# GpSimd's sums of the attention's P in instructions of 224 columns in place of 448

## The chip, the cores and the metric

The kernel runs on one core of a Trainium2 chip. The metric is the device time of one execution in microseconds; several executions are timed and their median is given. One execution was profiled, and the views below come from that one.

## What is computed

Three layers follow one another: attention with capped scores, a soft mixture of experts, and a two-layer MLP. The change lies in the attention.

```python
# q, k, v: (4, 12, 448, 64)   batch, heads, sequence, head size
scores = scale * np.matmul(q, k.transpose(0, 1, 3, 2))
scores = cap * np.tanh(scores / cap)
scores = scores - np.max(scores, axis=-1, keepdims=True)
attn = np.exp(scores)
attn = attn / (np.sum(attn, axis=-1, keepdims=True) + 1e-09)
attn_out = np.matmul(attn, v)
...
x = attn_out.transpose(0, 2, 1, 3).reshape(1792, 768)
x = soft_moe(x, phi, w1, w2)       # 8 experts of 4 slots, 768 -> 1024 -> 768
out = mlp(x, w_in, w_out, alpha)   # 768 -> 2048 -> 768, leaky rectifier
```

## The kernel before

**Attention.** The 48 heads are worked off as 24 pairs (`NPAIR`), i = 0 to 23. P is kept transposed, keys on the partitions and the 448 queries along the columns. The 448 keys are cut into three chunks of 128 (c = 0, 1, 2) and a tail of 64 (c = 3), whose two heads share one tile of 128 partitions. The order of the chunks is `CHUNKS = (0, 3, 1, 2)`.

The loop runs over steps g, four to a pair. In step g `qk` makes the scores of one chunk on TensorE (tile `s`, three products of a high and a low part) and ScalarE turns them into P: tanh (L408) and exp (L409), for both heads at once, 896 columns. Two steps later (`LAG = 2`) `pv` multiplies that P with V (tile `o`). Between them the background work of the step is issued (`run_bg`): row sums, normalisation, logits of the mixture, and so on.

**The sums of P.** The softmax needs the sum of P over all keys. GpSimd adds the chunks into a tile `acc` of 128 partitions, two heads `u` and 448 columns (`S`); `acc` has one buffer for even and one for odd pairs. In `pv` with c = 1 it adds chunks 0 and 1 (L425) and then the tail (L428, 64 partitions); with c = 2 it adds chunk 2 (L432). That is six instructions of 448 columns for a pair, and two for the last pair, whose other parts TensorE adds. `row_sums` (L440 on) then sums `acc` over the partitions with matmuls against `hot`, four calls of 224 columns (`HS`), two heads times two halves, into a tile `rs`; they are issued two steps after `pv` with c = 2. VectorE adds `rs` into `sums` (L459, L463), and after three pairs takes the reciprocal and splits it (L487 to L489), from which TensorE spreads `rb` and VectorE makes the normalised output `xn` out of `xu` (L513).

**What else VectorE does there.** For every pair it makes the parts of Q and K: `qh` (L387), `kl` (L374), `ql` (L388). For the MLP's weights `w_in`, which come as 64-bit numbers, it does a conversion in `to_f32` once in about four steps: ScalarE begins it (L203) and VectorE does four steps in place on 512 columns of `cvbuf`, L204, L208, L211 and L214; where they fall is set by a table of steps:

```python
cv_steps = [2, 5] + list(range(9, 58, J)) + [59] + list(range(61, 90, J))   # J = 4
```

For each batch (six pairs) it makes the softmax over slots, with a subtraction and a product in `c_all` (L694, L699) around an exp on ScalarE (L695).

**What sets the order.** TensorE's matmuls are chained in the order of the program text. The other engines' instructions are placed by the framework's scheduler out of the same text; each engine works its own list in order, and semaphores join them. GpSimd has nothing else to do in the attention but the sums.

**After the attention** come the experts, whose weights arrive by DMA from about 235 us on, and from about 330 us the MLP on TensorE.

Of the kernel before, what the change touches and what calls it, by code (L numbers as in the profile page):

```python
# [25 lines left out]
def tile_attention_soft_moe_mlp(ctx, tc, q, k, v, cap, phi, w1, w2, w_in, w_out, alpha, out):  # L26
    nc = tc.nc
    B, H, S, D = q.shape
# [12 lines left out]
    HS = S // 2  # L41
# [4 lines left out]
    JK = 3  # L46
# [205 lines left out]
    def attention():  # L252
        with ExitStack() as pools:
# [43 lines left out]
            nat, stk, sc_t, pt, acc, ov, xu, xn = {}, {}, {}, {}, {}, {}, {}, {}  # L297
# [7 lines left out]
            def matmul(*a, **kw):  # L305
                ins = nc.tensor.matmul(*a, **kw)  # L306
                if order:
                    if order[0] is not None:
                        tc.add_manual_dep(ins.ins, order[0].ins.name, NOSYNC, reason="tilings together")
                    order[0] = ins  # L310
                return ins
# [5 lines left out]
            def later(d, fn, *a):  # L317
                bg.setdefault(now[0] + d, []).append((fn, a))
# [93 lines left out]
            def pv(i, c):  # L412
                if c == 0:
                    ov[i] = ps_o.tile([128, 512], F32, tag="o", name="o")
                    acc[i] = acc_p[i % 2].tile([128, 2, S], F32, tag="acc", name="acc")
                o, a, t, pe = ov[i], acc[i], nat["v", i], pt[i, c]
                if i == NPAIR - 1 and c == 2:
                    row_sums(i)
                for u in range(2):
                    r = slice(TAIL * u, TAIL * u + TAIL)  # L420
                    lhsT, rhs = (t[r, 2 * JK, :], pe[r, 0, :]) if c == JK else (t[:, JK * u + c, :], pe[:, u, :])
                    matmul(o[64 * u:64 * u + 64, :S], lhsT, rhs, start=(c == 0), stop=(c == 2))
                if c == 1:
                    for u in range(2):
                        nc.gpsimd.tensor_add(out=a[:, u, :], in0=pt[i, 0][:, u, :], in1=pe[:, u, :])  # L425
                        r = slice(TAIL * u, TAIL * u + TAIL)
                        if i < NPAIR - 1:
                            nc.gpsimd.tensor_add(out=a[r, u, :], in0=a[r, u, :], in1=pt[i, JK][r, 0, :])  # L428
                if c == 2:
                    if i < NPAIR - 1:  # L430
                        for u in range(2):
                            nc.gpsimd.tensor_add(out=a[:, u, :], in0=a[:, u, :], in1=pe[:, u, :])  # L432
                    xu[i] = xu_p.tile([128, J * 128], F32, tag="xu", name="xu")[:, :S]
                    nc.scalar.activation(out=xu[i], in_=o[:, :S], func=AF.Copy)  # L434
                    if i < NPAIR - 1:
                        later(2 if i < NPAIR - 2 else 1, row_sums, i)
# [321 lines left out]
            for g in range(NPAIR * J + LAG):  # L758
                now[0] = g
                i, c = divmod(g, J)  # L760
                if g == 14:
                    nc.sync.dma_start(out=alpha_sb, in_=alpha.rearrange("(k p) -> p k", p=128))
                if g == 17:
                    nc.vector.tensor_scalar(out=nalpha_sb, in0=alpha_sb, scalar1=-1.0, scalar2=None, op0=ALU.mult)
                if i < NPAIR:
                    qk(i, CHUNKS[c])
                    if c == 1 and i + 1 < NPAIR:
                        trans_k(i + 1)
                        trans_q(i + 1)
                run_bg()  # L770
                if i < NPAIR:
                    if c == 0:
                        last = load(i + 2, "kq") or last
                    for n in range(ncv):
                        if cv_at(n) == g - 2:
                            store_w_in(n)
                        if cv_at(n) == g:
                            conv_w_in(n)
                if g >= LAG:
                    n, e = divmod(g - LAG, J)  # L780
                    pv(n, CHUNKS[e])
                    if e == J - 1:
                        load(n + 2, "v")
                if i < NPAIR and c == 1 and i in LOADS and may_load() is not None:
                    load_next(last)
            while bg:
# [10 lines left out]
                out=diag, in0=stackI[:, 0:NSLOT], scalar1=z_run, scalar2=None, op0=ALU.mult  # L797
# [668 lines left out]
```

## Time and profile before

| | |
|---|---|
| median of 3 runs | 583.16 us (581.52 to 583.71) |
| the profiled execution | 583.41 us, its span 581.6 us |
| TensorE busy | 550.8 us, 95% of the span |
| VectorE busy | 425.9 us, 73% |
| ScalarE busy | 387.3 us, 67% |
| GpSimd busy | 173.4 us, 30% |
| chain of waits, largest shares | TensorE 71%, DMA 14%, ScalarE 7%, VectorE 5% |
| granted TensorE clock | full in all of 40 slices |

In the profile PE is TensorE, DVE is VectorE, ACT is ScalarE, POOL is GpSimd and SP is SyncE. A share of the whole span says little here, since the three layers have different limits: GpSimd's 30% lie almost all in the first 248 us. A row of the timeline may stand for several like instructions (x2); its time is then from the first one's start to the last one's end. In brackets stands the idle time of the engine ahead of it and what ended it.

### The profile page before, as it was taken

The numbers are of one execution on the slowest core, as the hardware profiler recorded it, in microseconds if no ns is written. First come the engines' busy times: TensorE is split into PE (matmuls) and PEld (weight loads), VectorE is DVE, ScalarE is ACT, GpSimd is POOL, SyncE is SP. The second block draws the span as 40 slices with busy tenths as digits, with TensorE's granted clock in tenths as the row PEclk, the third lists the DMA queues.
The fourth block names the chain that finished last, engine by engine and source line by source line (L and its number), as shares of the span: only waits on it lengthen the run. The fifth ranks groups of instructions, "written<-read, shape, count | busy, mean of one in ns | idle before, by whom it ended". The sixth has DMA issues, their size and how long they took to land.

```text
span 581.6 us, 11121 instructions
## 1 busy us (share of the span) xinstructions
PE 550.8 (95%) x4204; PEld 388.7 (67%) x4204; DVE 425.9 (73%) x782; ACT 387.3 (67%) x612; POOL 173.4 (30%) x158
## 2 busy tenths in 40 slices
PE   5999999999999999999997899999999999999996
PEld 4444444455444544466664567878888999999996
DVE  3778767796999768661023379998999979797974
ACT  3999989898988878721012368985777755555551
POOL 0798786767595755600000000000000000000000
PEclk9999999999999999999999999999999999999999
DMA  7668788887878992899999999300120101010101
GB/s 176 155 134 252 215 256 260 259 257 205 256 218 222 319 280 58 310 398 415 419 414 420 389 395 416 141 1 1 54 56 1 54 2 55 1 55 2 54 1 54
DMA packets 83604, 110.93 MB, mean 191 GB/s; under 512 B 55392, under 2 KB 63328, under 8 KB 82016
## 3 DMA queue, kind: packets, MB, share of 16 engines
q1 hardware_dynamic: 81312, 109.28, 56.2%
q10 hardware_dynamic: 2240, 0.95, 0.6%
q8 instruction: 33, 0.54, 0.4%
q14 instruction: 19, 0.16, 0.1%
HBM read 98.41 MB, written 11.80 MB: 190 GB/s over the span
## 4 chain that ended last, share of the span: by engine, by line
PE 71%; DMA 14%; ACT 7%; DVE 5%; issue 1%; SPq 1%; ACTq 0%; DVEq 0%
PE o L306 10%; DMA w<-in_moe_w_dram 9%; PE s L306 9%; PE P L1280 7%; PE P L1278 7%; PE P L1279 7%; PE oc L1052 6%; PE oc L1053 6%; PE oc L1046 6%; DMA v<-in_v_dram 3%; PE aps L974 2%; PE nx L306 2%; ACT p L408 2%; ACT p L409 2%; PE rs L306 2%; PE tr L306 1%
## 5 line engine op out<-in xcount | busy, mean ns | idle before, releaser
L306 PE MATMUL o<-p,v 128*64 128x448 f32 (+1 forms) x384 | 93.3, 564 | 6.7 <-ACT xu L434 4.0
L408 ACT ACTIVATE p<-s 128x896 f32<-128x896 f32 x96 | 78.8, 821 | 22.6 <-PE s L306 19.6
L409 ACT ACTIVATE p<-p,cap 128x896 f32<-128x896 f32 x96 | 90.9, 948 | 2.3
L425 POOL TENSOR_TENSOR acc<-p 128x448 f32<-128x448 f32 x48 | 61.6, 1304 | 57.5 <-ACT p L409 57.4
L1052 PE MATMUL oc<-wsp,gr 128*128 128x512 f32 (+1 forms) x192 | 65.0, 339 | 0.3 <-DVE wsp L866 0.3
L1053 PE MATMUL oc<-wsp,gr 128*128 128x512 f32 (+1 forms) x192 | 64.3, 338 | 0.0
L1046 PE MATMUL oc<-wsp,gr 128*128 128x512 f32 (+1 forms) x192 | 63.7, 340 | 0.0
L306 PEld LDWEIGHTS s<-qh,kh 64*128 64x128 f32 (+1 forms) x168 | 18.2, 186 | 66.6 <-issue 25.4
L1269 ACT ACTIVATE gr<-gs 128x384 fp32r<-128x384 f32 (+1 forms) x64 | 36.8, 577 | 33.8 <-DVE gs L1253 27.8
L428 POOL TENSOR_TENSOR acc<-acc,p 64x448 f32<-64x448 f32 x46 | 55.4, 1205 | 1.7
L432 POOL TENSOR_TENSOR acc<-acc,p 128x448 f32<-128x448 f32 x46 | 53.4, 1181 | 1.8
L1270 DVE TENSOR_TENSOR gr<-gs,gr 128x384 fp32r<-128x384 f32 x64 | 39.1, 619 | 18.1 <-ACT gr L1269 18.1
L306 PE MATMUL s<-qh,kh 64*128 64x448 f32 (+1 forms) x168 | 46.0, 476 | 0.0
L1278 PE MATMUL P<-wsp,gr 128*128 128x384 f32 x128 | 42.9, 335 | 0.0
L1279 PE MATMUL P<-wsp,gr 128*128 128x384 f32 x128 | 42.8, 334 | 0.0
L1280 PE MATMUL P<-wsp,gr 128*128 128x384 f32 x128 | 42.8, 334 | 0.0
L1046 PEld LDWEIGHTS oc<-wsp,gr 128*128 128x128 f32 x192 | 36.3, 190 | 5.5 <-issue 0.6
L1052 PEld LDWEIGHTS oc<-wsp,gr 128*128 128x128 f32 x192 | 36.4, 189 | 5.2 <-DVE wsp L866 0.8
L306 PEld LDWEIGHTS o<-p,v 128*64 128x64 f32 (+1 forms) x384 | 19.0, 134 | 31.2 <-ACT xu L434 11.2
L1053 PEld LDWEIGHTS oc<-wsp,gr 128*128 128x128 f32 x192 | 36.3, 189 | 5.1 <-issue 0.8
L306 PE MATMUL s<-ql,kh 64*128 64x448 f32 (+1 forms) x168 | 35.6, 368 | 1.1 <-DVE ql L388 1.1
L306 PE MATMUL s<-qh,kl 64*128 64x448 f32 (+1 forms) x168 | 35.6, 367 | 0.0
(230 smaller groups left out, 1226.0 us busy)
## 6 DMA issues: line engine op xcount, KB each, us to landing
w<-in_moe_w_dram SPq DMA_DIRECT2D x25, 768.0 KB, 10.4
w<-in_moe_w_dram SPq DMA_DIRECT2D x12, 1536.0 KB, 11.3
cvbuf<-in_moe_w_in_dram SPq DMA_DIRECT2D x24, 512.0 KB, 5.5
w<-in_moe_w_out_dram SPq DMA_DIRECT2D x16, 768.0 KB, 10.8
w_in<-cvbuf SPq DMA_DIRECT2D x24, 256.0 KB, 3.3
w<-in_moe_w_dram SPq DMA_DIRECT2D x12, 512.0 KB, 6.4
w<-in_moe_w_dram SPq DMA_DIRECT2D x14, 384.0 KB, 4.9
q<-in_q_dram SPq DMA_DIRECT2D x44, 112.0 KB, 3.6
```

The costliest lines, as they stand in the source:

```text
L306: ins = nc.tensor.matmul(*a, **kw)
L408: nc.scalar.activation(out=pe, in_=ps[:, :n, :S], func=AF.Tanh)
L409: nc.scalar.activation(out=pe, in_=pe, func=AF.Exp, scale=cap_sb)
L425: nc.gpsimd.tensor_add(out=a[:, u, :], in0=pt[i, 0][:, u, :], in1=pe[:, u, :])
L428: nc.gpsimd.tensor_add(out=a[r, u, :], in0=a[r, u, :], in1=pt[i, JK][r, 0, :])
L432: nc.gpsimd.tensor_add(out=a[:, u, :], in0=a[:, u, :], in1=pe[:, u, :])
L1046: ins = nc.tensor.matmul(o, gh[:, ts], wo_h[f][:, cols], start=(f == 0 and not second), stop=False)
L1052: nc.tensor.matmul(o, gh[:, ts], wo_l[f][:, cols], start=False, stop=False)
L1053: nc.tensor.matmul(o, gl[:, ts], wo_h[f][:, cols], start=False, stop=(f == KF - 1 and not more))
L1278: nc.tensor.matmul(o, hi[:, i], bh, start=(p == 0), stop=False)
L1279: nc.tensor.matmul(o, hi[:, i], bl, start=False, stop=False)
L1280: nc.tensor.matmul(o, lo[:, i], bh, start=False, stop=(p == 7))
```

## The change

Every sum is split along its columns: 0 to 223 and 224 to 447. The same additions are made, on the same tiles.

```diff
                 o, a, t, pe = ov[i], acc[i], nat["v", i], pt[i, c]
+                halves = slice(0, HS), slice(HS, S)
...
                 if c == 1:
                     for u in range(2):
-                        nc.gpsimd.tensor_add(out=a[:, u, :], in0=pt[i, 0][:, u, :], in1=pe[:, u, :])
                         r = slice(TAIL * u, TAIL * u + TAIL)
+                        for f in halves:
+                            nc.gpsimd.tensor_add(out=a[:, u, f], in0=pt[i, 0][:, u, f], in1=pe[:, u, f])
                         if i < NPAIR - 1:
-                            nc.gpsimd.tensor_add(out=a[r, u, :], in0=a[r, u, :], in1=pt[i, JK][r, 0, :])
+                            for f in halves:
+                                nc.gpsimd.tensor_add(out=a[r, u, f], in0=a[r, u, f], in1=pt[i, JK][r, 0, f])
                 if c == 2:
                     if i < NPAIR - 1:
                         for u in range(2):
-                            nc.gpsimd.tensor_add(out=a[:, u, :], in0=a[:, u, :], in1=pe[:, u, :])
+                            for f in halves:
+                                nc.gpsimd.tensor_add(out=a[:, u, f], in0=a[:, u, f], in1=pe[:, u, f])
```

L425, L428 and L432 of before are L428, L431 and L436 of the changed kernel. On GpSimd's list the six sums of a pair, here pair 0, stand so before (`p` is a chunk of P, the number behind a name that of its buffer, and in brackets is the engine whose semaphore the instruction waits for):

```order
L425 TENSOR_TENSOR acc_295<-p_243,p_286 128x448 [waits Activation_49]
L425 TENSOR_TENSOR acc_295<-p_243,p_286 128x448
L428 TENSOR_TENSOR acc_295<-acc_295,p_258 64x448 [waits Pool_49] x2
L432 TENSOR_TENSOR acc_295<-acc_295,p_305 128x448 [waits Activation_49,Pool_49]
L432 TENSOR_TENSOR acc_295<-acc_295,p_305 128x448
```

and so in the changed kernel:

```order
L428 TENSOR_TENSOR acc_295<-p_243,p_286 128x224 [waits Activation_49]
L428 TENSOR_TENSOR acc_295<-p_243,p_286 128x224
L431 TENSOR_TENSOR acc_295<-acc_295,p_258 64x224 [waits Pool_49] x2
L428 TENSOR_TENSOR acc_295<-p_243,p_286 128x224 x2
L431 TENSOR_TENSOR acc_295<-acc_295,p_258 64x224 [waits Pool_49]
L431 TENSOR_TENSOR acc_295<-acc_295,p_258 64x224
L436 TENSOR_TENSOR acc_295<-acc_295,p_305 128x224 [waits Activation_49,Pool_49]
L436 TENSOR_TENSOR acc_295<-acc_295,p_305 128x224 x3
```

The first head is now finished with chunks 0, 1 and the tail before the second begins; before, both heads' chunks came first. Instructions that wait for GpSimd's own semaphore are four in place of three.

On TensorE's list, at the row sums of pair 0 (`rs`) between the scores and the product with V, before:

```order
L306 MATMUL s_390<-qh_275,kl_267 128x448 x2
L306 MATMUL rs_400<-acc_295,hot_136 32x224 [waits Pool_49]
L306 MATMUL rs_400<-acc_295,hot_136 32x224
L306 MATMUL rs_400<-acc_295,hot_136 32x224 [waits Pool_49]
L306 MATMUL rs_400<-acc_295,hot_136 32x224
L306 MATMUL o_386<-p_340,v_174 64x448
```

and in the changed kernel:

```order
L306 MATMUL s_396<-qh_275,kl_267 128x448 x2
L306 MATMUL rs_406<-acc_295,hot_136 32x224 [waits Pool_49] x4
L306 MATMUL o_392<-p_344,v_174 64x448
L306 MATMUL o_392<-p_344,v_174 64x448 [waits DMAHW4_49]
L306 MATMUL s_417<-qh_361,kh_352 128x448 [waits DVE_49,Activation_49]
```

The matmuls keep their place; each of the four calls now waits for its own quarter of `acc`, where each head's first call waited for that head's whole sum.

## Rows read from the trace of the kernel before

**Rows 1.** Busy time by stretch: engine, busy us, instructions; clock, DMA share, GB/s.

```profile
18.00:62.00 44.00, 41.07 (x261) 19.27 (x259) 36.03 (x47) 41.97 (x56) 39.04 (x31) 1.00 0.70 194
...
119.00:248.00 129.00, 124.71 (x946) 62.23 (x946) 105.01 (x174) 109.10 (x151) 87.80 (x74) 1.00 0.77 236
```

**Rows 2.** View by tile, acc: duration in ns, shortest/median/longest, first and last start.

```profile
L425 POOL TENSOR_TENSOR acc<-p x48: 1130/1263/1643, 18.9 to 245.9; 128x448 f32<-128x448 f32 x48
L428 POOL TENSOR_TENSOR acc<-acc,p x46: 1128/1144/1602, 22.0 to 237.7; 64x448 f32<-64x448 f32 x46
```

**Rows 3.** Timeline of VectorE, two conversions: start us, us, engine, line.

```profile
148.75 0.69 DVE L214 SCALAR_TENSOR_TENSOR cvbuf<-cvbuf 128x512 uint32<-128x512 uint32 x1
...
150.50 1.34 DVE L204 TENSOR_SCALAR cvbuf<-cvbuf 128x512 f32<-128x512 f32 x1 [0.17 <-ACT cvbuf L203]
...
154.70 1.51 DVE L214 SCALAR_TENSOR_TENSOR cvbuf<-cvbuf 128x512 uint32<-128x512 uint32 x1
```

**Rows 4.** Timeline of ScalarE: its waits for VectorE, in brackets.

```profile
122.06 0.31 ACT L695 ACTIVATE c_all<-c_all 112x128 f32<-112x128 f32 x1 [0.46 <-DVE c_all L694]
...
156.84 0.54 ACT L434 ACTIVATE xu<-o 128x448 f32<-128x448 f32 x1 [0.60 <-DVE xn L513]
...
183.27 0.31 ACT L695 ACTIVATE c_all<-c_all 112x128 f32<-112x128 f32 x1 [0.63 <-DVE c_all L694]
```

**Rows 5.** Timeline of GpSimd, pairs 0 to 3.

```profile
24.48 2.42 POOL L432 TENSOR_TENSOR acc<-acc,p 128x448 f32<-128x448 f32 x2
...
29.70 2.81 POOL L428 TENSOR_TENSOR acc<-acc,p 64x448 f32<-64x448 f32 x2
32.59 2.44 POOL L432 TENSOR_TENSOR acc<-acc,p 128x448 f32<-128x448 f32 x2
35.76 2.50 POOL L425 TENSOR_TENSOR acc<-p 128x448 f32<-128x448 f32 x2 [0.73 <-ACT p L409]
...
41.45 2.42 POOL L432 TENSOR_TENSOR acc<-acc,p 128x448 f32<-128x448 f32 x2
44.36 3.07 POOL L425 TENSOR_TENSOR acc<-p 128x448 f32<-128x448 f32 x2 [0.49 <-ACT p L409]
...
49.83 2.28 POOL L432 TENSOR_TENSOR acc<-acc,p 128x448 f32<-128x448 f32 x2
```

**Rows 6.** Timeline of TensorE: row-sum matmuls of pairs 0 to 3.

```profile
26.79 0.74 PE L306 MATMUL rs<-acc,hot 128*32 128x224 f32 x8
...
35.56 0.59 PE L306 MATMUL rs<-acc,hot 128*32 128x224 f32 x8
...
44.16 0.59 PE L306 MATMUL rs<-acc,hot 128*32 128x224 f32 x8
...
52.77 0.59 PE L306 MATMUL rs<-acc,hot 128*32 128x224 f32 x8
```

**Rows 7.** Timeline, last sums and row-sum matmuls of pairs 22 and 23.

```profile
238.94 2.25 POOL L432 TENSOR_TENSOR acc<-acc,p 128x448 f32<-128x448 f32 x2
...
242.52 0.58 PE L306 MATMUL rs<-acc,hot 128*32 128x224 f32 x8
...
244.76 2.27 POOL L425 TENSOR_TENSOR acc<-p 128x448 f32<-128x448 f32 x2 [3.57 <-ACT p L409]
...
247.86 0.59 PE L306 MATMUL rs<-acc,hot 128*32 128x224 f32 x8
```

**Rows 8.** GpSimd's copies of 32 columns: in the timeline; as a group (busy, mean ns).

```profile
15.80 0.66 POOL L249 COPY phi_rep<-phi 128x32 f32<-128x32 f32 x4 [14.50 <-DMA phi<-in_moe_phi_dram]
...
L249 POOL COPY phi_rep<-phi 128x32 f32<-128x32 f32 x4 | 0.7, 212 | 14.5 <-DMA phi<-in_moe_phi_dram 14.5
```

**Rows 9.** Groups of VectorE, 20 to 275 us: busy us, mean ns; idle before.

```profile
L387 DVE TENSOR_SCALAR qh<-tr,tscale 128x448 fp32r<-128x448 f32 x22 | 14.9, 679 | 17.9 <-PE tr L306 17.8
```

**Rows 10.** Timeline of VectorE: two later conversions' last steps.

```profile
161.06 1.52 DVE L214 SCALAR_TENSOR_TENSOR cvbuf<-cvbuf 128x512 uint32<-128x512 uint32 x1
...
171.36 1.52 DVE L214 SCALAR_TENSOR_TENSOR cvbuf<-cvbuf 128x512 uint32<-128x512 uint32 x1
```

## The prediction

> **What bounds the kernel now.** The view of busy time by stretches comes first [rows 1]. GpSimd is busy 39.04 of the 44 us from 18 to 62 and 87.80 of the 129 us from 119 to 248. Beside it TensorE is busy 41.07 of 44 and 124.71 of 129 us, ScalarE 41.97 and 109.10. So TensorE and ScalarE together set the pace of the attention part, and GpSimd can matter there in two ways: it is late with a sum that TensorE reads, or it holds VectorE up.
>
> The view by tile gives the length of a sum [rows 2]: median 1.26 us at L425 and 1.14 us at L428, shortest 1.13, longest 1.64. L428's sums have 64 partitions and are no shorter. Six sums make a pair of heads.
>
> The VectorE timeline shows how it is held up [rows 3]. The last step of a conversion takes 0.69 us at 148.75, when GpSimd is idle, and 1.51 us at 154.70, in the midst of sums: 0.82 us more. What that costs the pace is read from ScalarE's waits [rows 4]: 0.46 us for c_all at 122.06, 0.60 us for xn (which VectorE makes right behind that conversion) at 156.84, 0.63 us for c_all at 183.27.
>
> Whether GpSimd is late is seen by setting the end of a pair's last sum [rows 5] beside the row-sum matmuls that read it [rows 6]. Pair 0's sums end at 24.48 + 2.42 = 26.90 and the matmuls begin at 26.79: TensorE already waits there a little, by 0.11 us. Pair 1: 35.03 against 35.56, 0.53 us of slack. Pair 2: 43.87 against 44.16, 0.29. Pair 3: 52.11 against 52.77, 0.66. Between pair 0 and pair 3 GpSimd pauses for 0.73 and 0.49 us alone (in the brackets of rows 5), 1.22 us in all. Later it is early: from pair 6 on the smallest slack is pair 22's, 241.19 to 242.52, 1.33 us [rows 7].
>
> **The change, part by part.**
>
> *More instructions.* 140 sums become 280, twelve in place of six a pair. Each added instruction pays once more what does not depend on columns. No row shows a sum of 224 columns, so I bound that price. Lower end: nothing, if the time goes by columns alone; below nothing is out, since the columns stay the same. Upper end: the whole of a copy of 32 columns, 0.21 us by its mean length; four of them take 0.66 us, so 0.165 us each by spacing [rows 8]. I take 0.15 us, just under the spacing, since 32 columns cost something too. A half sum is then (1.14 + 0.15)/2 = 0.65 us, and a pair grows by 6 x 0.15 = 0.9 us. In the order shown above, a pair's instructions wait for GpSimd's own semaphore four times in place of three; the pause of 32.59 - 29.70 - 2.81 = 0.08 us is what one such wait shows [rows 5]. So the growth is 1.0 us a pair, between 0.1 and 1.4.
>
> The Trainium skill, Perfetto Trace Analysis, section GPSIMD Engine Instruction, says to time this engine by start-to-start spacing and to distrust the length that the profiler reports. By the reported 0.21 us the loss below would be 3.3 us, by the spacing it is the 1.9 us that I take.
>
> *What the lateness costs.* After pair n the sums are later by (n + 1) x growth, less the pauses that GpSimd had until then. TensorE has the pair's slack, and about 0.24 us more: each of the eight matmul instructions waits for its own quarter of the sums, as the second order view shows, and of the 0.59 us that they take [rows 6] some 0.24 lie ahead of the last quarter's. Pair 0: 1.0 + 0.11 - 0.24 = 0.87. Pair 1: 2.0 - 0.53 - 0.24 = 1.23. Pair 2: 3.0 - 0.73 - 0.29 - 0.24 = 1.74. Pair 3: 4.0 - 1.22 - 0.66 - 0.24 = 1.88. Beyond it the pauses outrun the growth. The loss is the largest of these, **1.9 us**, and it passes whole, since in those 44 us TensorE has 3 and ScalarE 2 us of idle time only. At a growth of 0.1 us it is 0; at 1.36 us it is 4 x 1.36 - 2.1 = 3.3 us.
>
> In pairs 6 to 22 a growth of 1.0 us stays under the 1.33 us of slack [rows 7]: cost nothing, hidden behind TensorE's own work; with a growth over 1.33 us, a few tenths. Pair 23 has two sums in place of six, grows by 0.3 us and has 247.86 - 247.03 = 0.83 us [rows 7]: nothing.
>
> *Shorter waits on VectorE.* If a step that meets a sum waits for its end, a sum of 0.65 in place of 1.14 us shortens it by 0.5 us. The conversion from 150.50 on has four such steps, 2.0 us, but ScalarE behind it was held for 0.60 us [rows 4]; its own work is next in line. The two waits for c_all lose 0.46 and 0.5 us. Together **1.6 us**. The other shortened steps end in VectorE's own pauses: it stands 17.8 us in all for the transposes ahead of its 22 steps qh [rows 9].
>
> *New meetings.* GpSimd ends a pair 1 us later, and a conversion that now starts just behind it meets a half sum or two, at most 0.35 us each. The same 17.8 us, 0.8 us a pair, hide that; without them it would be up to 0.7 us in each such pair.
>
> *What does not move.* The instructions of TensorE, VectorE, ScalarE and SyncE keep their order.
>
> **Sum.** +1.9 - 1.6 = +0.3 us against the profiled execution of 583.41 us (its span is 581.6, the rest lies around it): **583.7 us**. That execution lies 0.25 us over the median of the runs, 583.16, which I leave to the range. A measurement of this kernel can tell about 0.5%, 2.9 us, from no change; so the forecast is no change.
>
> **Rivals.**
>
> *GpSimd becomes the bound of the first pairs (slower).* Its place is pairs 0 to 3 [rows 5, 6]. The loss follows 4 x growth - 2.1 us; with VectorE's gain of 1.6 us taken off it passes 2.9 us once a pair grows by 1.65 us, some 0.26 us for each added instruction. For it: only 5 of the 44 us are left to GpSimd [rows 1]. Against: the copy's 0.165 us. At 0.25 to 0.3 us it gives about 587 us. Chance 0.14.
>
> *VectorE slips in more often (slower).* A sum can take 1.60 in place of 1.14 us [rows 2], 0.46 us more, where a VectorE step got ahead of it. With twice as many joints twice as many steps may. Two more a pair in pairs 0 to 3 bring the growth to 1.9 us, the loss to 5.5, the time to 587.3. Against: VectorE has no more steps than before. Chance 0.05. The Trainium skill, SBUF — State Buffer, section Who interferes with whom, states that whoever issues first holds the ports that the two share for its whole instruction, so that either can block the other; the 1.51 beside 0.69 us agree for VectorE.
>
> *VectorE is the real bound from 150 to 173 us (faster).* Besides the four steps from 150.50, five more are as long between 159 and 173, the last of them at 171.36 [rows 10]. Nine times 0.5 us are gained, and with a growth of 0.7 us only 0.8 are lost: 583.4 - 4.5 + 0.8 = 579.7 us. Against: 0.60 us in that stretch is all that ScalarE waited for such a step [rows 4]. Chance 0.13.
>
> *It does nothing.* Both the growth and the gain are hidden: 583.4 us. Chance 0.12.
>
> **How the numbers follow.** The forecast has the remaining 0.56. Within 0.5%: 0.56 + 0.12 = 0.68; slower 0.14 + 0.05 = 0.19; faster 0.13. The range takes in the ends of the fixed price (a loss of 0 to 3.3 us), gains of 0.5 to 2.6 us, and the nearer part of each rival: 580.8 to 587.0 us.
>
> **What would show it.** Half sums of about 0.65 us; TensorE waiting for acc at rs in pairs 0 to 3 and no more by pair 6; L214 at some 1.0 us where it meets a sum; ScalarE's waits for c_all near nothing. A half sum of 0.7 us or more, or waits at rs beyond pair 6, speak for the first rival, a full sum's worth of GpSimd delay in more than two sums a pair for the second. A time under 580.5 us would say that VectorE's waits cost far more than ScalarE's rows show, and a time over 586.5 that the growth was priced too low.

## The result, and the profile after

The changed kernel is **slower**: 588.34 us in the median of 4 runs (587.12 to 588.99) against 582.71 for the kernel before in the same series (581.52 to 583.71). The ratio is 1.0085, 95% interval 1.0068 to 1.0103. The forecast was 583.7 us, its range ended at 587.0. The profiled execution took 587.12 us (span 585.1).

The half sums themselves came out as forecast. Groups of GpSimd after [rows 2]; the columns are busy us and mean ns of one, then idle time before:

```profile
L428 POOL TENSOR_TENSOR acc<-p 128x224 f32<-128x224 f32 x96 | 72.5, 774 | 34.8 <-ACT p L409 34.6
L436 POOL TENSOR_TENSOR acc<-acc,p 128x224 f32<-128x224 f32 x92 | 63.7, 724 | 1.8
L431 POOL TENSOR_TENSOR acc<-acc,p 64x224 f32<-64x224 f32 x92 | 59.9, 670 | 1.8
```

The undisturbed ones take 0.65 us, as the 1.28 us for two below show; the means are higher by the meetings with VectorE. Timeline of GpSimd, pairs 6 (last sums), 7 and 8 (first sums):

```profile
78.62 2.27 POOL L436 TENSOR_TENSOR acc<-acc,p 128x224 f32<-128x224 f32 x3
80.97 2.07 POOL L428 TENSOR_TENSOR acc<-p 128x224 f32<-128x224 f32 x2
83.00 1.27 POOL L431 TENSOR_TENSOR acc<-acc,p 64x224 f32<-64x224 f32 x2
84.25 1.28 POOL L428 TENSOR_TENSOR acc<-p 128x224 f32<-128x224 f32 x2
85.60 1.28 POOL L431 TENSOR_TENSOR acc<-acc,p 64x224 f32<-64x224 f32 x2
86.96 2.90 POOL L436 TENSOR_TENSOR acc<-acc,p 128x224 f32<-128x224 f32 x4
90.03 1.97 POOL L428 TENSOR_TENSOR acc<-p 128x224 f32<-128x224 f32 x2 [0.17 <-ACT p L409]
```

Timeline of VectorE, the conversion steps in the same stretch [rows 3]:

```profile
78.92 0.65 DVE L204 TENSOR_SCALAR cvbuf<-cvbuf 128x512 f32<-128x512 f32 x1
79.60 0.77 DVE L208 TENSOR_SCALAR cvbuf<-cvbuf 128x512 uint32<-128x512 uint32 x1
80.40 1.04 DVE L211 SCALAR_TENSOR_TENSOR cvbuf<-cvbuf 128x512 uint32<-128x512 uint32 x1
81.48 1.03 DVE L214 SCALAR_TENSOR_TENSOR cvbuf<-cvbuf 128x512 uint32<-128x512 uint32 x1
...
87.98 0.55 DVE L204 TENSOR_SCALAR cvbuf<-cvbuf 128x512 f32<-128x512 f32 x1
```

Read the two together. A held-up L214 takes 1.03 in place of 1.51 us, as forecast. But six of the seven conversions from 60 to 120 us now begin while L436 still runs and end in L428 of the next pair, and each of their steps lengthens a half sum. Pair 7's twelve take from 80.97 to 89.86, 8.89 us, and the first of pair 8 waits 0.17 us for P. In the kernel before pair 7's six took 7.34 us, and pair 8 had a pause of 2.51 us ahead of it; its timeline of GpSimd:

```profile
80.03 2.69 POOL L425 TENSOR_TENSOR acc<-p 128x448 f32<-128x448 f32 x2 [1.62 <-ACT p L409]
...
85.12 2.25 POOL L432 TENSOR_TENSOR acc<-acc,p 128x448 f32<-128x448 f32 x2
89.88 2.37 POOL L425 TENSOR_TENSOR acc<-p 128x448 f32<-128x448 f32 x2 [2.51 <-ACT p L409]
```

Counted over all 96 conversion steps (a step is held up when it is over 0.1 us longer than the shortest of its line): before 26, by 0.73 us each; now 50, by 0.34 us each. Between 60 and 120 us it was 5 of 27 and is 23 of 28. In all VectorE loses hardly less than before, some 17 us for 19, and GpSimd is met twice as often.

TensorE's row sums then wait. Timeline, pairs 0, 3, 4, 6, 7 and 10 [rows 6]:

```profile
25.14 0.57 PE L306 MATMUL rs<-acc,hot 128*32 128x224 f32 x4
26.16 0.57 PE L306 MATMUL rs<-acc,hot 128*32 128x224 f32 x2 [0.45 <-POOL acc L436]
27.23 0.57 PE L306 MATMUL rs<-acc,hot 128*32 128x224 f32 x2 [0.51 <-POOL acc L436]
...
53.22 0.58 PE L306 MATMUL rs<-acc,hot 128*32 128x224 f32 x6
54.15 0.56 PE L306 MATMUL rs<-acc,hot 128*32 128x224 f32 x2 [0.35 <-POOL acc L436]
62.90 0.58 PE L306 MATMUL rs<-acc,hot 128*32 128x224 f32 x8
...
80.65 0.87 PE L306 MATMUL rs<-acc,hot 128*32 128x224 f32 x8
89.72 0.76 PE L306 MATMUL rs<-acc,hot 128*32 128x224 f32 x8
...
120.23 0.59 PE L306 MATMUL rs<-acc,hot 128*32 128x224 f32 x8
```

Eight of them take 0.87 and 0.76 in pairs 6 and 7, where 0.59 is undisturbed. In the view of waits from 15 to 252 us (total us, times, longest) the row sums' weight loads and matmuls now wait for L436 and L428, where a single wait of 0.3 us stood before:

```profile
PEld rs L306 <- POOL acc L436: 4.4, 7, 0.9
ACT c_all L699 <- DVE c_all L698: 2.9, 2, 1.5
PE rs L306 <- POOL acc L436: 1.8, 4, 0.5
PEld rs L306 <- POOL acc L428: 1.4, 2, 0.7
```

The second line is the other place: c_all's wait was to shrink from 1.1 us to nothing and grew to 2.9. Timeline of GpSimd, VectorE and ScalarE there [rows 4]:

```profile
121.40 1.28 POOL L431 TENSOR_TENSOR acc<-acc,p 64x224 f32<-64x224 f32 x2
122.64 1.32 POOL L428 TENSOR_TENSOR acc<-p 128x224 f32<-128x224 f32 x2
...
121.58 1.87 DVE L698 TENSOR_TENSOR c_all<-dl,mx 112x128 f32<-112x128 f32 x1
...
123.48 0.31 ACT L699 ACTIVATE c_all<-c_all 112x128 f32<-112x128 f32 x1 [1.37 <-DVE c_all L698]
...
183.35 2.04 DVE L698 TENSOR_TENSOR c_all<-dl,mx 112x128 f32<-112x128 f32 x1
...
185.43 0.31 ACT L699 ACTIVATE c_all<-c_all 112x128 f32<-112x128 f32 x1 [1.52 <-DVE c_all L698]
```

The subtraction does not wait for one half sum: it overlaps both of L431 and reaches into those of L428, 1.87 us, though each is only 0.65 us long.

Last, TensorE's granted clock. Stretches in the experts (engines' busy us and instructions, clock, DMA share, GB/s), after:

```profile
264.00:266.00 2.00, 2.00 (x21) 1.52 (x24) 1.02 (x4) 0.00 (x0) 0.31 (x1) 0.80 0.99 385
266.00:268.00 2.00, 2.00 (x27) 0.95 (x23) 1.03 (x5) 0.31 (x1) 0.00 (x0) 0.50 1.04 418
268.00:270.00 2.00, 1.96 (x26) 0.95 (x18) 0.00 (x0) 0.33 (x1) 0.00 (x0) 0.85 1.02 410
```

It fell to 0.50, the lower of its two levels (1.2 of 2.4 GHz); before, it stood at 1.00 in these stretches.

Set against the profile of before, from one row-sum start to another (the two programs begin pair 0's at 25.14 and 26.79, a difference from ahead of the first sums, so I count from there):

| from row sums of pair | before | after | difference |
|---|---|---|---|
| 0 to 4 | 35.37 | 37.76 | +2.39 |
| 4 to 6 | 18.61 | 17.75 | -0.86 |
| 6 to 10 | 38.93 | 39.58 | +0.65 |
| 10 to 11 (c_all) | 9.26 | 10.13 | +0.87 |
| 11 to 13 | 20.34 | 20.34 | 0 |
| 13 to 16 | 31.44 | 31.30 | -0.14 |
| 16 to 17 (c_all) | 9.41 | 10.30 | +0.89 |
| 17 to the end of attention (tile si) | 69.70 | 69.71 | 0 |
| si to the end of the experts (tile yt) | 66.25 | 67.66 | +1.41 |

The first two rows are net figures. In the kernel before TensorE waits twice for a load of V: 0.76 us ahead of the row sums of pair 4, and 1.20 us, at 79.06, ahead of those of pair 6. Its view of waits from 15 to 252 us, and its timeline at the first of the two:

```profile
PE o L306 <- DMA v<-in_v_dram: 2.0, 2, 1.2
```

```profile
60.45 0.97 PE L306 MATMUL o<-p,v 128*64 128x448 f32 x4 [0.76 <-DMA v<-in_v_dram]
```

The changed kernel has neither wait; at the same two matmuls TensorE waits 0.15 us each for ScalarE, 1.66 us less in all. Against that stand 3.8 us lost at row sums: in pair 0 they take 2.66 us (25.14 to 27.80) in place of 0.74, in pair 3 1.49 (53.22 to 54.71) in place of 0.59, and in pairs 2 and 5 to 8 some 0.2 to 0.3 us more each. So pairs 0 to 4 lost 3.0 us, of which the first wait took 0.6 back, and the -0.86 from pair 4 to 6 is the second wait, not a faster sum. Why V's loads come in time there no run shows.

### The profile page after: what moved, and what is told of

Its sections match the earlier page's. It is cut to its first block, busy times and chain, and to the rows that moved or that the text cites. A ratio compares the mean times of both kernels' runs of the same rounds, so it can differ in the third digit from the quotient of the medians.

```text
span 585.1 us, 11261 instructions
## 1 busy us (share of the span) xinstructions
PE 552.7 (94%) x4204; PEld 388.5 (66%) x4204; DVE 420.8 (72%) x782; ACT 386.4 (66%) x612; POOL 198.4 (34%) x298
## 4 chain that ended last, share of the span: by engine, by line
PE 71%; DMA 11%; ACT 9%; DVE 4%; POOL 2%; issue 2%; SPq 1%; ACTq 0%; DVEq 0%; POOLq 0%
PE o L306 10%; DMA w<-in_moe_w_dram 9%; PE s L306 8%; PE P L1282 7%; PE P L1284 7%; PE P L1283 7%; PE oc L1056 6%; PE oc L1057 6%; PE oc L1050 6%; ACT p L409 3%; ACT p L408 3%; PE rs L306 2%; PE aps L978 2%; PE nx L306 2%; ACT cvbuf L203 1%
## 5 line engine op out<-in xcount | busy, mean ns | idle before, releaser
L428 POOL TENSOR_TENSOR acc<-p 128x224 f32<-128x224 f32 x96 | 72.5, 774 | 34.8 <-ACT p L409 34.6
L436 POOL TENSOR_TENSOR acc<-acc,p 128x224 f32<-128x224 f32 x92 | 63.7, 724 | 1.8
L431 POOL TENSOR_TENSOR acc<-acc,p 64x224 f32<-64x224 f32 x92 | 59.9, 670 | 1.8
L387 DVE TENSOR_SCALAR qh<-tr,tscale 128x448 fp32r<-128x448 f32 x23 | 15.7, 683 | 29.8 <-PE tr L306 29.7
```

The lines of the kernel that those rows point to most:

```text
L428: nc.gpsimd.tensor_add(out=a[:, u, f], in0=pt[i, 0][:, u, f], in1=pe[:, u, f])
L431: nc.gpsimd.tensor_add(out=a[r, u, f], in0=a[r, u, f], in1=pt[i, JK][r, 0, f])
L436: nc.gpsimd.tensor_add(out=a[:, u, f], in0=a[:, u, f], in1=pe[:, u, f])
```

## The experiments

Theory A: two places of the attention, each with its own price. In pairs 0 to 10 the longer sums come to lie under VectorE's conversions, these lengthen them further, and TensorE waits for the sums, some 2.1 us net; behind pairs 11 and 17 c_all's subtraction waits for several half sums, some 1.7 us. What the experts lose comes on top. The rivals stand in each expectation. The times of one series are compared with the kernel before of the same series: 583.79 us for the first four kernels, 583.12 for the next four, 583.02 for the last four. The table sums up the profiles, counted as above; 92.91 and 140.15 us are before's.

| kernel | median, us | ratio (95%) | pair 0 to 10 | pair 10 to si |
|---|---|---|---|---|
| changed kernel again | 588.07 | 1.0064 (1.0040 to 1.0087) | +2.09 | +1.62 |
| order_old | 587.33 | 1.0052 (1.0033 to 1.0072) | +1.83 | +0.21 |
| ballast | 586.86 | 1.0051 (1.0033 to 1.0069) | +2.26 | +0.12 |
| psum_after | 586.87 | 1.0046 (1.0030 to 1.0062) | +2.07 | +0.20 |
| noconv_before | 580.84 | 0.9953 (0.9935 to 0.9971) | -1.76 | -1.34 |
| noconv_after | 582.33 | 0.9986 (0.9970 to 1.0002) | -1.84 | +0.44 |
| psum_before | 583.19 | 0.9991 (0.9973 to 1.0009) | -0.02 | -0.11 |
| wide | 591.52 | 1.0146 (1.0121 to 1.0172) | +3.21 | +4.82 |
| early | 585.88 | 1.0033 (1.0014 to 1.0052) | +2.27 | +0.01 |
| late | 585.52 | 1.0039 (1.0016 to 1.0061) | -0.41 | +1.64 |
| half_first | 584.56 | 1.0021 (1.0003 to 1.0039) | +0.33 | -0.04 |
| half_last | 581.85 | 0.9978 (0.9957 to 1.0000) | -0.65 | -0.72 |

**again.** The changed kernel, unaltered.

> The changed kernel once more, for a second profile. Theory A (two places: VectorE's subtraction for c_all waits through three or four half sums in a row, and in pairs 0 to 10 the conversions now meet sums in every pair, so that GpSimd is busy some 8.9 of 9.0 us a pair and TensorE waits for it): 1.005 to 1.011 of the time before, L698 at 1.9 to 2.0 us in two places again, TensorE short of the sums in most of pairs 2 to 8. Theory B (only the price of the added instructions in pairs 0 to 3): rs on time from pair 4 on. Theory C (chance of TensorE's clock: it rose earlier at the start of the changed kernel's profile and fell to half for 3.4 us at 265 us): the fall is not there and the ratio lies under 1.006.

Measured: 588.07 us. The attention repeats the changed kernel's profile to 0.1 us, waits and all. The clock fell again, but elsewhere, from some 323 us on, just behind a wait of 2.11 us for weights:

```profile
318.69 1.50 PE L906 MATMUL h<-w,slotT 128*32 128x256 f32 x24 [1.34 <-DMA w<-in_moe_w_dram]
...
322.31 1.71 PE L906 MATMUL h<-w,slotT 128*32 128x256 f32 x24 [2.11 <-DMA w<-in_moe_w_dram]
```

So the attention's +3.7 us belongs to the kernel; the place of the fall does not. The first line is a wait for weights that the kernel before does not have at this matmul: there, with the clock still full, the experts were already 1.3 us later than before, counted from si.

**order_old.** Half sums, in the kernel before's order: both heads' chunks first, then the tails.

```diff
                     for u in range(2):
-                        r = slice(TAIL * u, TAIL * u + TAIL)
                         for f in halves:
                             nc.gpsimd.tensor_add(out=a[:, u, f], in0=pt[i, 0][:, u, f], in1=pe[:, u, f])
+                    for u in range(2):
+                        r = slice(TAIL * u, TAIL * u + TAIL)
                         if i < NPAIR - 1:
```

> Half sums, but both heads' chunks 0 and 1 ahead of both tails, as before the change; as many instructions. If the subtraction for c_all waits so long because a tail of 64 partitions stands ahead of other half sums (its idle half of the lanes runs on into the next), L698 falls to 0.7 to 0.9 us, ScalarE's waits there to under 0.5 us, and the time is 1.5 to 2 us less than the changed kernel's. If it is only that half sums follow each other without a joint, L698 stays at 1.3 us or more and the time within 0.7 us of the changed kernel's.

Measured: c_all's loss is gone (+0.21 for +1.62), that of the first pairs stays. The group of the subtraction, c_all <- dl, mx, and ScalarE's behind it:

```profile
L699 DVE TENSOR_TENSOR c_all<-dl,mx 112x128 f32<-112x128 f32 x3 | 1.7, 576 | 0.1
...
L700 ACT ACTIVATE c_all<-c_all 112x128 f32<-112x128 f32 x3 | 0.9, 311 | 0.5 <-DVE c_all L699 0.3
```

Here the same subtraction got in among four half sums of L427 that follow each other, after 0.64 and 0.81 us. So the long wait does not come from the sums' length alone; whether their order decides, or the moment at which the subtraction falls among them, this run does not separate (half_first below has both a long and a short one in the order of the changed kernel). The time fell by only 0.7 us where 1.5 to 2 were expected, within the two kernels' spread.

**ballast.** Whole sums, and behind each a sum of 8 columns into a tile that nothing reads; the sums stay long, the instructions are as many as in the changed kernel.

```diff
-                        for f in halves:
-                            nc.gpsimd.tensor_add(out=a[:, u, f], in0=pt[i, 0][:, u, f], in1=pe[:, u, f])
+                        nc.gpsimd.tensor_add(out=a[:, u, :], in0=pt[i, 0][:, u, :], in1=pe[:, u, :])
+                        nc.gpsimd.tensor_add(out=ballast[:, u], in0=pt[i, 0][:, u, :8], in1=pe[:, u, :8])
```

> The kernel before with whole sums, and behind each a GpSimd sum of 8 columns into unused room, so that GpSimd grows by about the same 0.9 to 1.1 us a pair while a sum still holds VectorE up for 1.14 us. If the growth of GpSimd is the loss (theory A, second place): slower than before by as much as the changed kernel or more, 5 to 9 us, since each of the added meetings costs 0.83 in place of 0.36 us. If the loss came from half sums following each other at c_all alone: within 2 us of before.

Measured: +2.26 us in pairs 0 to 10, as much as halves cost there, though not a single sum is shorter. 49 conversion steps are held up, by 0.79 us each: the number of the changed kernel at nearly the price of before. So short sums are not needed for the meetings: it is enough that GpSimd is busy longer in each pair (8.7 to 9.0 us from the first sum into `acc` to the last in pairs 2 to 10), or that it has more joints. The 5 to 9 us that were expected did not come, it was 3.1: VectorE's longer steps seem to be largely covered. c_all's subtraction takes 0.29 us at both places here, beside one of the small sums.

**psum_after.** The changed kernel; c_all's max and subtraction read the logits from PSUM, so that the subtraction has one input in SBUF.

```diff
-                later(1, softmax_c, b)
+                later(1, softmax_c, b, ps.rearrange("p (j s) -> p j s", j=J)[:, :, NSLOT:2 * NSLOT])
```

> The changed kernel, with the subtraction and the maximum for c_all reading the logits from PSUM, where they come from, in place of the copy in SBUF: one SBUF input less. If L698's wait is one for the SBUF side that GpSimd uses, it falls to 0.3 us, ScalarE does not wait for it at the two places, and the time is 2 to 3 us less than the changed kernel's. If it waits for something else, nothing changes.

Measured: the subtraction takes 0.28 us at both places, behind pair 17 in the midst of a half sum, and ScalarE waits for it no more:

```profile
L699 ACT ACTIVATE c_all<-c_all 112x128 f32<-112x128 f32 x3 | 0.9, 299 | 0.1
...
L698 DVE TENSOR_TENSOR c_all<-nd,mx 112x128 f32<-112x128 f32 x3 | 0.8, 282 | 0.0
```

The attention's second part gets back 1.42 us of its 1.62, the time 1.2 us, where 2 to 3 were expected. So it was the read of SBUF that waited. The Trainium skill, SBUF — State Buffer, section Who interferes with whom, says that a VectorE instruction with two SBUF inputs contends with a GpSimd instruction that reads SBUF, and that one with at most one does not, outside the 2-port perf modes: 0.28 against 1.87 us agrees. The conversion's L204, with one input in SBUF, was held up too (1.34 us at 150.50 in [rows 3]); whether it runs in such a mode no run shows.

**noconv_before and noconv_after.** Each kernel without VectorE's four conversion steps.

```diff
         def to_f32 ...
+        if after:
+            tc.add_manual_dep(first.ins, after[0].ins.name, NOSYNC, reason="not before its step")
+            return
```

> The kernel before without VectorE's four steps of each conversion of w_in (the MLP's input weights are then stored as ScalarE's first step leaves them, so the conversion is left out). It is the partner of noconv_after and has whole sums of 448 columns. Theory A (VectorE's conversion steps and the sums lengthen each other): clean pairs, 6.9 to 7.1 us of sums in nearly every pair in place of up to 8.1, and 0.5 to 1.5 us less than the kernel before, since ScalarE's wait of 0.60 us for xn and the small waits of pairs 0 to 3 go. Theory B (only GpSimd's own time counts): about the same, within 0.5 us, since TensorE waited for a sum only 0.1 us in pair 0.

> The changed kernel with the same conversion steps left out. Theory A: without those steps a pair's twelve half sums take 7.8 to 8.3 us against periods of 8.6 to 9.0 us, so TensorE's waits for acc at rs (7.7 us in all in the changed kernel) fall to under 1 us, and what is left over noconv_before at the end of the attention is c_all's subtraction, 1.7 us (1.2 to 2.2), in place of 3.75. Theory B (GpSimd is too slow by its own fixed price, met or not): the waits at rs stay at several us and the attention ends 3.2 to 4 us later than in noconv_before. If the fall of TensorE's clock in the experts goes with the halves, either adds some 1.2 us behind the attention.

Measured: without conversions a pair of whole sums takes 6.9 us, a pair of half sums 7.7 to 7.9, and pairs 0 to 10 take 91.15 and 91.07 us: **the growth alone costs nothing there**. Of the waits only c_all's is left, with two short ones at row sums:

```profile
ACT c_all L702 <- DVE c_all L701: 2.9, 2, 1.5
...
PEld rs L309 <- POOL acc L431: 1.4, 2, 0.7
```

The pair differs by 1.70 us up to si (230.0 in place of 231.7), which is c_all, and by 1.5 us in the medians, where the full kernels differ by 4.3 (again). That is theory A's number; its rival wanted 3.2 to 4. noconv_before also shows how much the conversions cost the kernel before: 3.1 us of the attention, of which 2.3 reach the time, more than the 0.5 to 1.5 expected. The 1.76 us up to pair 10 are TensorE's two waits for V, which noconv_before does not have; noconv_after has neither.

**psum_before.** The kernel before with c_all from PSUM; the edit is psum_after's.

> The kernel before (whole sums) with c_all's max and subtraction reading the logits from PSUM. Theory A (the subtraction waits because both its inputs and the sums lie on one side that VectorE and GpSimd share): the subtraction takes 0.28 to 0.3 us in place of 1.04 to 1.23, ScalarE's two waits of 0.46 and 0.63 us for it go, 0.5 to 1.1 us less than the kernel before, so about 582.3 us where that has 583.2. Theory C (those waits are hidden, since a later one takes their place): the same time within 0.3 us.

Measured: ScalarE's two waits of 0.46 and 0.63 us are gone, the time is the same. Theory C holds: the two waits for c_all that I had priced as gains were nearly all hidden (0.1 us in the second part).

**wide.** The other direction: chunks of both heads in sums of 896 columns.

```diff
+                    nc.gpsimd.tensor_add(out=a, in0=pt[i, 0], in1=pe)
...
-                        for u in range(2):
-                            nc.gpsimd.tensor_add(out=a[:, u, :], in0=a[:, u, :], in1=pe[:, u, :])
+                        nc.gpsimd.tensor_add(out=a, in0=a, in1=pe)
```

> The other direction: chunks 0, 1 and 2 of both heads are added in sums of 896 columns, so a pair has four instructions (two of 896, two of 448 for the tail) in place of six. Theory A (length of a sum sets what a blocked VectorE step loses, number of joints sets how many steps get in): sums of about 2.1 us, a clean pair of 6.6 us, no wait of TensorE at rs beyond pair 0; but blocked steps of conversions up to 2.3 us and c_all's subtraction up to 2.2 us, so ScalarE waits longer for c_all and xn, by 1 to 2 us in all: 584 to 585.5 us where the kernel before has 583.2. Theory B (only GpSimd's own time counts): 0 to 0.3 us less than the kernel before.

Measured: 591.52 us, 8.4 more, far beyond theory A's 1 to 2. Fewer steps are held up (21, none of 26 between 60 and 120 us), by 1.22 us each, but at two places they stop everything. Timeline of VectorE and TensorE at the first:

```profile
58.50 2.45 DVE L214 SCALAR_TENSOR_TENSOR cvbuf<-cvbuf 128x512 uint32<-128x512 uint32 x1
60.87 0.44 DVE L458 TENSOR_SCALAR sums<-rs,guard 128x224 f32<-128x224 f32 x1
...
61.37 0.86 PE L306 MATMUL tr<-ident,q 112*128 112x112 f32 x4 [3.49 <-DVE sums L458]
```

Four steps take 6.8 us in a row, the addition of `rs` behind them is late, and TensorE stands 3.49 us for it; then its clock is at 0.50 from 62 to 64 us. So a longer sum is not cheaper either, and the price of a held-up step is not a constant: little of TensorE's time where something covers it, 3.49 us here.

**early and late.** Half sums in pairs 0 to 10 alone, and from pair 11 on alone.

```diff
-                halves = slice(0, HS), slice(HS, S)
+                halves = (slice(0, HS), slice(HS, S)) if i < 11 else (slice(0, S),)
```

> The changed kernel with half sums in pairs 0 to 10 alone, whole sums (in the changed kernel's order) from pair 11 on. Theory A (two places, each with its price: TensorE waits for late sums in pairs 0 to 8, 2.1 us; c_all's subtraction behind half sums in pairs 11 and 17, 1.75 us): row sums of pair 10 begin 2 us (1.6 to 2.4) later than in the kernel before, ScalarE's waits for c_all stay at 1.1 to 1.3 us, so the attention ends 2 to 2.4 us later. Theory B (all is the early pairs' lateness): the attention ends 3.7 us later. Theory C (all that is real is c_all, the rest is where the clock stood): it ends 0 to 0.5 us later. If the clock's fall in the experts goes with half sums, 1.2 us more behind it.

> The reverse: whole sums in pairs 0 to 10, half sums from pair 11 on. Theory A: pair 10's row sums within 0.2 us of the kernel before, set from pair 0 on; then the two periods behind pairs 11 and 17 grow by 0.85 us each, and the attention ends 1.75 us later (1.4 to 2.1), 0.3% of the time. Theory B: no later. Theory C: 1.75 us later.

Measured: the two prices come apart as theory A has them. Their row sums of pairs 0 and 10 and si, early, then late:

```profile
26.10 0.57 PE L306 MATMUL rs<-acc,hot 128*32 128x224 f32 x4
...
121.28 0.59 PE L306 MATMUL rs<-acc,hot 128*32 128x224 f32 x8
...
261.44 1.20 PE L306 MATMUL si<-phi_rep,s_run 128*128 128x32 f32 x6
```

```profile
26.10 0.88 PE L306 MATMUL rs<-acc,hot 128*32 128x224 f32 x8
...
118.60 0.59 PE L306 MATMUL rs<-acc,hot 128*32 128x224 f32 x8
...
260.39 1.20 PE L306 MATMUL si<-phi_rep,s_run 128*128 128x32 f32 x6
```

Early loses 2.27 us to pair 10 and nothing behind it; late loses nothing to pair 10 (-0.41, it has one of the two waits for V, 1.18 us) and 1.64 us behind it. The medians, +2.9 and +2.5 us, add up to 5.4, the changed kernel's loss within the intervals. Theories B and C, of one place each, are out.

**half_first and half_last.** Halves for chunks 0, 1 and the tail alone, or for chunk 2 alone.

```diff
-                        nc.gpsimd.tensor_add(out=a[:, u, :], in0=pt[i, 0][:, u, :], in1=pe[:, u, :])
+                        for f in halves:
+                            nc.gpsimd.tensor_add(out=a[:, u, f], in0=pt[i, 0][:, u, f], in1=pe[:, u, f])
```

> Halves for chunks 0, 1 and the tail (L425, L428 of the kernel before), whole sums for chunk 2. A clean pair grows by 0.6 us in place of 0.9. Theory A: c_all's subtraction falls among the same half sums as in the changed kernel, 1.87 and 2.05 us, so its 1.75 us stay whole; the lateness in pairs 0 to 8 shrinks to 0.5 to 1.3 us: attention 2.3 to 3 us later. Theory B (lateness alone): 0.5 to 1.5 us later.

> Halves for chunk 2 alone (L432 of the kernel before), the other four sums of a pair whole and in the order of before. A clean pair grows by 0.3 us. Theory A: c_all's subtraction meets the same whole sums as in the kernel before, so its waits stay at 1.1 us in all; lateness in pairs 0 to 3 of 0 to 0.6 us: the same time as before within 1 us. Theory B: 0.3 to 1 us later. With halves_first it should add up to less than the changed kernel, since lateness sets in only when the pauses are used up.

Measured: half_first loses 0.3 us in the attention in place of 2.3 to 3. c_all's subtraction takes 1.95 us behind pair 11 as in the changed kernel, but 0.29 us behind pair 17: there it begins 0.07 us ahead of a joint, at 180.52 us, with the next sum at 180.59. Theory A's "stays whole" was wrong there. Its +0.33 up to pair 10 is net of the two waits for V, which it does not have. half_last gains 1.4 us in the attention and 1.2 in the median; its interval ends at 1.0000, so it beats the changed kernel, and the kernel before perhaps. Its conversion steps are held up 34 times by 0.60 us. It loses 1.0 us at pair 0's row sums, and what it gains up to pair 10 is the two waits for V: its best stretch, pair 5 to 6, 8.78 us in place of 9.84, is the kernel before without the wait of 1.20 us. half_last is the only kernel with all of the computation that came out under the kernel before by more than 0.2%.

## Why the prediction was wrong

- *More instructions*: right. 0.65 us for a half sum, growth 0.8 to 1.0 us a clean pair (noconv_after against noconv_before) where 1.0 stood.
- *What the lateness costs*, +1.9 us in pairs 0 to 3: the net of +2.4 comes near it by luck. Pair 0 alone lost 1.92 us in place of 0.87, since a conversion lay over its last sums and its twelve took 9.79 us for 8.01; pair 3 added 0.90. And the loss did not pass "whole": 0.6 of 3.0 us fell into a wait for V that TensorE had before. The growth does all this only together with the conversions: noconv_after has the growth without them and loses nothing.
- "In pairs 6 to 22 a growth of 1.0 us ... cost nothing", and *New meetings*, "17.8 us ... hide that": **wrong**. I covered the meetings with VectorE's idle time, yet the other side pays too: each meeting lengthens a half sum, by 0.2 us (0.85) or 0.45 (1.1). With four a pair, pair 7 grew by 1.55 us in place of 1.0 (8.89 for 7.34), and its slack at the row sums went from 2.19 us to -0.14; TensorE loses some 0.8 us at the row sums of pairs 5 to 8 where nothing stood, +0.65 from pair 6 to 10. This was the second rival's mechanism (VectorE slips in more often), held at 0.05 with "VectorE has no more steps than before". The steps are no more; those that meet a sum doubled, since the sums now lie where they fall.
- *Shorter waits on VectorE*, -1.6 us: **the largest miss, and of the wrong sign**. "The two waits for c_all lose 0.46 and 0.5 us" became +0.87 and +0.89: 2.7 us of the error. Two things failed. That a step waits for the end of one sum is not what L698 does: 1.87 and 2.04 us, over several half sums. And the waits for c_all were no gain to be had: psum_before has none of them and the same time. For xn, pairs 13 to 16 gained 0.14 in place of 0.60: the row sums of pair 14 begin 1.07 us sooner, those of pair 15 lose 1.18 again, since pair 14's half sums meet conversions and take 10.0 us.
- Not foreseen: +1.41 us in the experts, whose cause is open. The clock's fall made TensorE 1.6 us late by 268.4 us, but it is not shown to be the loss. Again, the same kernel, was 1.3 us late by a wait for weights ahead of its fall, and two kernels without any fall there lose by the same wait: psum_before 1.53 us over the stretch (a wait of 1.62 us at 313.35), early 0.75 (0.81 us at 316.00). The DMA share from 260 to 318 us is 1.02 in the kernel before and in again, and in all of these profiles TensorE waits for weights near the end of the stretch. That points to their arrival as the bound, with or without the fall; why they arrive later no run shows. The fall stands in seven of seven profiles with halves in pair 23, in two of the seven others (noconv_before, wide). It came at 261 to 265 us in five of the seven, with TensorE busy 8.95 of the 9 us from 255 to 264 in the changed kernel (8.99 in the kernel before, where it did not fall), and behind a wait for weights in the other two. Why it falls stays open.

Sum by these steps: forecast +1.9 - 1.6 = +0.3; measured, from pair 0's row sums on, +2.2 in pairs 0 to 10 (3.8 at row sums less 1.7 of waits for V) and +1.6 behind them, with 1.4 in the experts, 5.2 us; the medians differ by 5.6.

## What to carry to other kernels

Where two engines hold each other up, work out for each step which instructions of the other will lie under it after the change, and charge both sides: idle time of one is no cover for the other. A wait of an engine that the trace shows is only worth what is behind it; remove it alone before counting it as a gain. A time between two marks can come out near the forecast because a loss met a wait that was there before: compare the waits too, not the sum alone. And before splitting an instruction to let another engine in sooner, look whether the waiting one can do with operands that don't meet at all, as c_all's subtraction could (1.87 to 0.28 us).

## What the runs showed that I had not expected

- A VectorE subtraction with both inputs in SBUF waited through several of GpSimd's sums in a row, 1.87 and 2.04 us with sums of 0.65 us; in another order of like sums it got in after 0.64 and 0.81. What decides at a joint was not found.
- 49 and 50 held-up conversion steps with sums of 1.14 us plus small ones (ballast) and of 0.65 us (changed kernel) cost TensorE the same, 2.26 and 2.18 us up to pair 10, though VectorE lost 0.79 and 0.34 us a step.
- Sums of 896 columns, fewer and with less time in all, cost 8.4 us through two places where TensorE stood for VectorE, the first for 3.49 us.
